# Weight maxima of two experts read from resident tiles, v's peeks two steps later, and a chunk's maximum set apart from its transposition

## The chip, the cores and the metric

One core of a Trainium2 chip runs one launch. The metric is device microseconds from the first to the last instruction of an execution, as the median of three runs. Five engines work side by side, each through its own queue and in the order of that queue: PE (TensorE, matrix products), DVE (VectorE), ACT (ScalarE), POOL (GpSimd) and SP, whose queue issues all transfers (DMAs) of this kernel. An instruction that has to wait holds back everything that stands behind it in its queue.

## What is computed

Causal attention with a decay per key for 4 batches of 8 heads (576 positions, 64 wide), and behind it a dense mixture of 4 experts over all 2304 tokens:

```python
scores = scale * np.matmul(q, k.transpose(0, 1, 3, 2))
scores = np.where(causal, -1000000000.0, scores + decay)
attn = softmax(scores)                      # over the keys
x = np.matmul(attn, v)                      # as 2304 tokens x 512
p = domain_probs / (domain_probs.sum(-1, keepdims=True) + 1e-09)
for e in range(4):
    h = np.maximum(x @ w1[e], 0.0)          # 512 -> 1024
    out += p[:, e:e + 1] * (h @ w2[e])      # 1024 -> 512
```

## The kernel before

**Chunks and steps.** The tokens are cut into 9 chunks of 256. Chunks 0 to 3 are the first 256 positions of a batch each, and chunks 4 to 8 share the other 320 positions of the four batches. The experts' work is a list of 80 steps. A step takes one chunk through two weight tiles (a tile is 128 hidden units of one expert, both matrices, 128x1024): `l1` (24 products, line 976) into PSUM, `gate` (ReLU into `gh` on ACT and the remainder `gl` on DVE, line 990), and one step later `l2` (12 products, line 1008); every second step DVE adds two PSUM tiles to `acc` (line 1031). Tile names carry the step as sweep, group, chunk and half: `l1_1_0_3_0` is the first half of group 0 of the second sweep for chunk 3. Steps 0 to 27 are the first sweep, with 32-bit tiles `wh` and `wl`, in which chunks 0, 1 and 2 go through the experts as they become ready. Steps 28 to 79 are the second sweep, in which chunks 1 to 4 go through with 16-bit halves; chunk 3 comes first in step 32 and chunk 4 in step 40. Chunks 5 to 8 follow in a last part (from about 650 us) with a scheme of their own, which the change does not touch.

**Attention beside the steps.** Attention for later chunks is a second list (`asteps`). Each entry has a cost, and `pace` hands entries out between the steps in proportion to these costs, so that a chunk is done three steps before its first use; `upto` hands out whatever is still missing when a step needs its chunk. For a head this is `s` (scores, line 608), a maximum on DVE (622), `p` (exponential on ACT, 637), for the second half of the positions `z` (16-bit halves, 702 and 703) and a transposing DMA from `z` to `pt` (708), and then `o` (attention times v, 783). When a chunk is complete, `turn(c)` finds its scale: `top` (a maximum over 128x1024 on DVE, line 257), `across` (a transposition on PE into `topx`, 196), `exponent` (DVE, and a second small product into `topx`, 217) and `finish` (DVE). `narrow` then makes the chunk's 16-bit halves `y` (ACT 471, DVE 472), which the second sweep's `l1` reads.

**Scales of weights and of v.** The second sweep also needs a power of two for each expert's two matrices and for v. Before, each expert gets 16 steps of `w_peek` (line 278): one DMA of 256 KB from HBM into `pk`, of which there is a single buffer, and one step later a maximum over it on DVE (281). `PEEK = (1, 15, 31, 45)` gives the first step for each expert. Then `w_scale` writes 128x2 maxima to HBM (`dw`) and reads them back to all partitions (`tops`, one buffer). For v there are ten `v_peek` steps (DMA of 512 KB into `vp`, maximum on ACT, 352) from step `V_PEEK = 1` on, and `v_scale` goes through HBM in the same way (`dv`, line 370, and `tops`, line 371).

```python
def w_peek(e, i):
    n, k = divmod(i, 2)
    t = pk_p.tile([128, 512], F32, tag="pk", name=f"pk{e}_{i}")
    nc.sync.dma_start(out=t, in_=w[8 * e + n, :, 512 * k : 512 * k + 512])
    at_step(step + 1, lambda: nc.vector.tensor_reduce(
        out=wmax[:, k, n, e : e + 1], in_=t, op=ALU.max, ...))
```

**What sets the order.** The program hands its instructions to a scheduler, which orders them for each engine before the launch (only the start-up part is ordered by hand). The order is then fixed. `w_split(n)` (line 897 issues the load of `wr`) turns a loaded tile into `wh` on ACT (line 916) and `wl` on DVE or POOL (920); in the first sweep tiles 16 to 23 are expert 2's (third) and 24 to 31 expert 3's (fourth), and all of them pass through SBUF there.

Of the kernel before, what the change touches and what calls it, by code (L numbers as in the profile page):

```python
# [8 lines left out]
F32 = mybir.dt.float32  # L9
# [4 lines left out]
ALU = mybir.AluOpType  # L14
AX = mybir.AxisListType
# [12 lines left out]
    ((1, 2, 3, 4), (1, 2, 3, 4), (2, 3, 4), (3, 4)),  # L28
)
WIDE = (0, 1, 2)  # L30
PEEK = (1, 15, 31, 45)
V_PEEK = 1
TURN = ((1, 14), (2, 18), (3, 24), (4, 28))
LEAD = 3
W_DVE = tuple(range(0, 16, 2))
# [41 lines left out]
def fused(ctx: ExitStack, tc: tile.TileContext, qk, v, f, probs, w, out):  # L77
    nc = tc.nc
# [35 lines left out]
    wmax = const.tile([128, 2, 8, E], F32, name="wmax")  # L114
# [72 lines left out]
    def at_step(n, f):  # L187
        later.setdefault(n, []).append(f)
# [54 lines left out]
    def x_scale(k, cols):  # L243

        def use(u, r):
            nc.vector.tensor_scalar(
                out=xsc[:, k : k + 1], in0=r, scalar1=2.0**2, scalar2=None, op0=ALU.mult
            )
            nc.vector.tensor_scalar(
                out=xun[:, k : k + 1], in0=u, scalar1=2.0**-2, scalar2=None, op0=ALU.mult  # L250
            )
            known.add(("x", k))

        def top():
            for i, c in enumerate(cols):
                x = xh[c].bitcast(F32) if c in WIDE else xf[c]
                nc.vector.tensor_reduce(
                    out=xmax[:, k + i : k + i + 1],
                    in_=x,
                    op=ALU.max,  # L260
                    axis=AX.XY,
                    apply_absolute_value=True,
                )
            n = len(cols)
            if n > 1:
                nc.vector.tensor_reduce(
                    out=xmax[:, k + n : k + n + 1], in_=xmax[:, k : k + n], op=ALU.max, axis=AX.X
                )

        n = k + len(cols) if len(cols) > 1 else k  # L270
        across, exponent, finish = power(1, xmax[:, n : n + 1], f"x{k}", use)
        return top, across, exponent, finish

    def w_peek(e, i):
# [8 lines left out]
            ),  # L283
        )

    def w_scale(e):

        def use(u, r):
            for k in range(2):
                nc.vector.tensor_scalar(  # L290
                    out=wsc[:, e, k : k + 1],
                    in0=r[:, k : k + 1],
                    scalar1=(2.0**2, 2.0**14)[k],
                    scalar2=None,
                    op0=ALU.mult,
                )
            nc.vector.scalar_tensor_tensor(
                out=wun[:, e : e + 1],
                in0=u[:, :1],
                scalar=2.0**-16,  # L300
                in1=u[:, 1:],
                op0=ALU.mult,
                op1=ALU.mult,
            )
            known.add(("w", e))

        m = st_p.tile([128, 2], F32, tag="wm", name=f"wm{e}", bufs=2)
        d = dr_p.tile([128, 2], F32, tag="dw", name=f"dw{e}", bufs=2)
        u = st_p.tile([128, 4], F32, tag="uw", name=f"uw{e}", bufs=2)

        def top():
            nc.vector.tensor_reduce(out=m, in_=wmax[:, :, :, e], op=ALU.max, axis=AX.X)
            nc.sync.dma_start(out=d, in_=m)
            nc.sync.dma_start(
                out=tops, in_=d.rearrange("q k -> (q k)").partition_broadcast(128)
            )

        def finish():
            nc.vector.tensor_reduce(
                out=u[:, :2],  # L320
                in_=tops.rearrange("p (q k) -> p k q", k=2),
                op=ALU.max,
                axis=AX.X,
            )
            nc.vector.tensor_scalar(
                out=u[:, :2], in0=u[:, :2], scalar1=TINY, scalar2=None, op0=ALU.max
            )
            nc.vector.tensor_scalar(
                out=u[:, :2].bitcast(I32),
                in0=u[:, :2].bitcast(I32),  # L330
                scalar1=EXPONENT,
                scalar2=None,
                op0=ALU.bitwise_and,
            )
            nc.vector.reciprocal(out=u[:, 2:], in_=u[:, :2])
            use(u[:, :2], u[:, 2:])

        return top, finish
# [141 lines left out]
    def turn(c):  # L480

        top, across, exponent, finish = x_scale(c, (c,))
        return [
            (50, lambda: (top(), across())),
            (50, exponent),
            (150, finish),
        ]

    class Job:
# [401 lines left out]
    wh, wl, wraw = {}, {}, {}  # L891
# [14 lines left out]
    def w_split(n):  # L906
        if n >= NS:
            if n % 2 == 0:
                big_split((n - NS) // 2)
            return  # L910
        w_load(n)
        r = wraw.pop(n)
        if n < 32:
            wh[n] = w_p.tile([128, 1024], F32R, tag="wh", name=f"wh{n}")
            wl[n] = w_p.tile([128, 1024], F32R, tag="wl", name=f"wl{n}")
            nc.scalar.activation(out=wh[n], in_=r, func=AF.Copy)  # L916
            eng = nc.vector if n in W_DVE else nc.gpsimd
            for a in (0, 512):
                z = a + 512
                eng.tensor_tensor(  # L920
                    out=wl[n][:, a:z],
                    in0=r[:, a:z],
                    in1=wh[n][:, a:z].bitcast(F32),
                    op=ALU.subtract,
                )
        else:
            e = n % 32 // 8
            assert ("w", e) in known
            t = w_pair(f"w{n}")
            wh[n], wl[n] = t[:, 0], t[:, 1]  # L930
            for k in range(2):
                c = slice(512 * k, 512 * k + 512)
                sc = wsc[:, e, k : k + 1]
                if k == 1:
                    nc.gpsimd.tensor_scalar(
                        out=r[:, c], in0=r[:, c], scalar1=sc, scalar2=None, op0=ALU.mult
                    )
                    nc.scalar.activation(out=wh[n][:, c], in_=r[:, c], func=AF.Copy)
                    nc.gpsimd.tensor_tensor(
                        out=wl[n][:, c], in0=r[:, c], in1=wh[n][:, c], op=ALU.subtract  # L940
                    )
                    continue
                nc.scalar.activation(out=wh[n][:, c], in_=r[:, c], func=AF.Copy, scale=sc)
                nc.vector.scalar_tensor_tensor(  # L944
                    out=wl[n][:, c],
                    in0=r[:, c],
                    scalar=sc,
                    in1=wh[n][:, c],
                    op0=ALU.mult,
                    op1=ALU.subtract,  # L950
                )
            at_step(step + 2, lambda: nc.sync.dma_start(out=wd[n - 32], in_=t))
        w_load(n + 1)
        w_load(n + 2)
        w_load(n + 3)
# [141 lines left out]
    def big_split(p):  # L1097
        if p >= 16:
            return
        r = wr_p.tile([128, 2, 512], F32, tag="wr", name=f"wr{NS + p}")  # L1100
        nc.sync.dma_start(
            out=r, in_=w[2 * p : 2 * p + 2, :, :512].rearrange("n p c -> p n c")
        )
        bw[p] = [w_pair(f"bw{p}_{k}") for k in range(3)]
        for k in range(2):
            nc.sync.dma_start(out=bw[p][k], in_=wd[2 * p + k])
        part = lambda b: r[:, b[0], 256 * b[1] : 256 * b[1] + 256]
        t = late.x.tile([128, 4, 256], F32, tag="wt", name=f"wt{p}", bufs=2)
        w_of = lambda b: part(b) if type(b) is tuple else t[:, b - 1, :]
        for k, a, z, op in SUMS:  # L1110
            nc.gpsimd.tensor_tensor(out=t[:, k - 1, :], in0=w_of(a), in1=w_of(z), op=op)
        f = t.rearrange("p k n -> p (k n)")
        hi, lo = bw[p][2][:, 0], bw[p][2][:, 1]
        nc.scalar.activation(out=f, in_=f, func=AF.Copy, scale=wsc[:, p // 4, 0:1])
        nc.scalar.activation(out=hi, in_=f, func=AF.Copy)  # L1115
        for a in (0, 512):
            z = a + 512
            nc.gpsimd.tensor_tensor(out=lo[:, a:z], in0=f[:, a:z], in1=hi[:, a:z], op=ALU.subtract)  # L1118
# [216 lines left out]
    prev, step = None, 0  # L1335
# [9 lines left out]
    for n in range(len(W_SLOT), 6):  # L1345
        w_split(n)

    used = set()
    for n in range(len(steps) + 1):
        step = n  # L1350
        cur = steps[n] if n < len(steps) else None
        for f_ in later.pop(n, ()):
            behind(f_)
        for e, first_ in enumerate(PEEK):
            if 0 <= n - first_ < 16:
                w_peek(e, n - first_)
            if n == first_ + 17:
                a_, b_ = w_scale(e)
                behind(a_)
                at_step(n + 3, b_)  # L1360
        if 0 <= n - V_PEEK < NV:
            v_peek(n - V_PEEK)
        if n == V_PEEK + NV + 1:
            a_, b_ = v_scale()
# [84 lines left out]
```

## Time and profile before

| | us |
|---|---|
| median of 3 runs | 965.07 |
| lowest and highest | 962.48 and 970.98 |
| the profiled execution | 969.94 |
| its span (first to last instruction) | 968.2 |
| mean granted TensorE clock in it | 0.981 of full speed |

The profile is that of one execution. Its time, 969.94 us, is 1.74 us more than its span, and 4.87 us above the median of the three runs. Times in the rows below count from the start of the span. Where a row says "A <- B", A's engine stood idle and B is what it waited for.

### The profile page before, as it was taken

What the parts mean: (1) busy time and instruction counts of PE and PEld (TensorE: products, weight loads), DVE (VectorE), ACT (ScalarE), POOL (GpSimd) and SP (SyncE); (2) the same over time, 40 slices, a digit from 0 to 9 for tenths busy, and PEclk for the clock granted to TensorE, in tenths of its full rate; (3) what the DMA queues carried; (4) which work ended last, traced back from release to release, by engine and by line L of the source; (5) the groups of instructions that cost most, each with busy time, mean ns of one, the idle gap of its engine ahead of it and who ended that gap; (6) DMA issues with size and microseconds to landing.
All of it is one profiled execution on the core that took longest, in us unless ns stands there. A gap on an engine that the chain in (4) does not pass through costs nothing.

```text
span 968.2 us, 15252 instructions
## 1 busy us (share of the span) xinstructions
PE 908.9 (94%) x5311; PEld 597.8 (62%) x5311; DVE 716.0 (74%) x1460; ACT 493.2 (51%) x983; POOL 441.6 (46%) x464
## 2 busy tenths in 40 slices
PE   4799998999989969899899989999999999999998
PEld 3699888999766647566566757654444444444443
DVE  5776775787978969789788878577666766676665
ACT  5777746466756748566666666454223222221110
POOL 4666955567624845425653564484233223320000
PEclk9999998999999969999999989999999999999999
DMA  7458753738987888975996599534122222121002
GB/s 245 141 200 288 263 125 132 207 109 288 256 194 180 228 191 209 275 156 141 278 345 141 111 257 292 121 120 151 65 87 75 100 66 81 50 66 44 1 1 88
DMA packets 130350, 154.13 MB, mean 159 GB/s; under 512 B 84868, under 2 KB 87616, under 8 KB 130272
## 3 DMA queue, kind: packets, MB, share of 16 engines
q1 hardware_dynamic: 130272, 153.14, 55.7%
q8 instruction: 42, 0.69, 0.3%
q14 instruction: 36, 0.29, 0.1%
HBM read 112.06 MB, written 21.65 MB: 138 GB/s over the span
## 4 chain that ended last, share of the span: by engine, by line
PE 58%; DMA 14%; DVE 12%; ACT 6%; POOL 5%; issue 4%; SPq 1%; ACTq 0%; DVEq 0%; POOLq 0%
PE y L1191 17%; PE m L1133 15%; PE l L1008 10%; PE l L976 9%; DMA pk<-in_w 4%; DMA raw<-in_qk 3%; DMA pt<-z 3%; PE s L608 3%; PE o L783 3%; DMA wr<-in_w 2%; DVE z L703 2%; DVE wmax L281 1%; DVE p L622 1%; DVE w L944 1%; ACT p L637 1%
## 5 line engine op out<-in xcount | busy, mean ns | idle before, releaser
L976 PE MATMUL l<-y,w 128*128 128x256 f16 x1248 | 157.2, 275 | 1.0 <-DVE y L472 1.0
L1191 PE MATMUL y<-bw,hh 128*128 128x512 f16 x512 | 152.3, 379 | 0.0
L637 ACT ACTIVATE p<-p,nm 128x576 f32<-128x576 f32 (+2 forms) x160 | 95.6, 598 | 93.3 <-DVE nm L622 93.0
L1133 PE MATMUL m<-rh,bw 128*128 128x512 f16 x448 | 139.3, 379 | 0.0
L976 PEld LDWEIGHTS <-w 128*128 128x128 f16 x1248 | 118.5, 99 | 33.4 <-issue 8.9
L1031 DVE SCALAR_TENSOR_TENSOR acc<-y,scg,acc 128x512 f32<-128x512 f32 x120 | 89.4, 749 | 59.7 <-PE y L1191 58.9
L1008 PE MATMUL l<-w,gh 128*128 128x512 f16 x416 | 127.3, 386 | 6.0 <-DVE acc L1031 6.0
L1118 POOL TENSOR_TENSOR bw<-wt,bw 128x512 f16<-128x512 f32 x32 | 36.7, 1171 | 176.4 <-ACT bw L1115 176.4
L1133 PEld LDWEIGHTS <-bw 128*128 128x128 f16 x672 | 65.7, 98 | 79.3
L1191 PE MATMUL y<-bw,hl 128*128 128x512 f16 x256 | 96.9, 379 | 0.0
L703 DVE SCALAR_TENSOR_TENSOR z<-p,z 128x384 f16<-128x384 f32 (+3 forms) x128 | 82.0, 661 | 17.9 <-ACT z L702 16.4
L608 PE MATMUL s<-hi 128*128 128x384 f32 (+1 forms) x192 | 77.5, 407 | 16.3 <-DVE hi L570 8.7
L1150 DVE TENSOR_TENSOR u<-m,u 128x512 f32<-128x512 f32 x96 | 65.7, 689 | 31.2 <-PE m L1133 29.3
L1191 PEld LDWEIGHTS <-hh 128*128 128x128 f16 x512 | 50.1, 98 | 60.4
L556 POOL CAST q<-raw 64x320 fp32r<-64x320 f32 (+1 forms) x56 | 26.4, 471 | 132.1 <-PE s L608 72.7
L1133 PE MATMUL m<-rl,bw 128*128 128x512 f16 x224 | 84.9, 379 | 0.0
L622 DVE CUSTOM_DVE_ANT_0 p<-s,mask 128x288 f32<-128x288 f32 (+2 forms) x160 | 74.5, 475 | 10.4 <-PE s L608 9.4
L1008 PE MATMUL l<-w,gl 128*128 128x512 f16 x208 | 79.5, 385 | 0.0
L1159 ACT ACTIVATE hh<-u 128x512 f16<-128x512 f32 x64 | 39.3, 626 | 78.5 <-DVE u L1150 78.5
L564 POOL TENSOR_TENSOR kl<-raw,hi 64x576 fp32r<-64x576 f32 (+1 forms) x56 | 66.9, 1195 | 25.6 <-ACT hi L555 25.5
L920 POOL TENSOR_TENSOR wl<-wr,wh 128x512 fp32r<-128x512 f32 x48 | 64.9, 1377 | 16.9 <-ACT wh L916 10.5
L990 DVE SCALAR_TENSOR_TENSOR gl<-l,gh 128x512 f16<-128x512 f32 (+1 forms) x80 | 54.7, 684 | 16.9 <-ACT gh L989 16.6
(154 smaller groups left out, 2031.3 us busy)
## 6 DMA issues: line engine op xcount, KB each, us to landing
wr<-in_w SPq DMA_DIRECT2D x80, 512.0 KB
pk<-in_w SPq DMA_DIRECT2D x64, 256.0 KB
wd<-w SPq DMA_DIRECT2D x32, 512.0 KB
bw<-wd SPq DMA_DIRECT2D x32, 512.0 KB
raw<-in_qk SPq DMA_DIRECT2D x16, 896.0 KB
raw<-in_qk SPq DMA_DIRECT2D x12, 512.0 KB
vp<-in_v SPq DMA_DIRECT2D x10, 512.0 KB
vr<-in_v SPq DMA_DIRECT2D x16, 320.0 KB
```

The source lines that it names most:

```text
L564: eng.tensor_tensor(out=kl[:64, :wk], in0=r[:64, ko : ko + wk], in1=hi[:64, ko : ko + wk].bitcast(F32), op=ALU.subtract,)
L608: nc.tensor.matmul(out=ps[:, at : at + z - a], lhsT=lhsT, rhs=rhs, start=(m == 0), stop=(m == 1),)
L622: nc.vector.tensor_tensor_reduce(out=pt[:, a:z], in0=ps, in1=mask[:, m0 + a : m0 + z], scale=-0.125, scalar=BIG if n == 0 else nm[:, col : ...
L637: nc.scalar.activation(out=pt[:, :w_], in_=pt[:, :w_], func=AF.Exp, scale=-1.0, bias=self.nmax[hh][:, c : c + 1], accum_out=self.ssum[:, h ...
L703: nc.vector.scalar_tensor_tensor(out=o[:, 1], in0=x, scalar=2.0**14, in1=o[:, 0], op0=ALU.mult, op1=ALU.subtract)
L920: eng.tensor_tensor(out=wl[n][:, a:z], in0=r[:, a:z], in1=wh[n][:, a:z].bitcast(F32), op=ALU.subtract,)
L976: nc.tensor.matmul(out=self.l1p[:, fi, :], lhsT=lhsT, rhs=rhs[:, k, :], start=(k == 0 and m == 0), stop=(k == 3 and m == 2),)
L1008: nc.tensor.matmul(out=l2[tt], lhsT=lhsT, rhs=rhs, start=(self.ps == 0 and fi == 0 and m == 0), stop=(self.ps == 1 and fi == 1 and m == 2),)
L1031: nc.vector.scalar_tensor_tensor(out=acc[c][:, tt, :], in0=ps, scalar=sc, in1=acc[c][:, tt, :], op0=ALU.mult, op1=ALU.add,)
L1133: nc.tensor.matmul(out=ps, lhsT=lhsT[:, o], rhs=rhs[:, k, :], start=(k == 0 and i == 0), stop=(k == 1 and i == 2),)
L1150: nc.vector.tensor_tensor(out=out, in0=a, in1=z, op=op)
L1191: nc.tensor.matmul(out=ps, lhsT=lhsT, rhs=rhs, start=(fi == 0 and m == 0), stop=(fi == 1 and m == 2),)
```

## The change

1. `PEEK` has only two entries, for experts 0 and 1. For experts 2 and 3 the 32 DMAs of 256 KB and their 32 maxima over 128x512 are gone. In their place `w_stat(n)` takes the maximum over the resident tile `wh[n]` (128x1024, two results) two steps after the tile is split, 16 times in all, and after the last tile of an expert `w_scale` follows.
2. `V_PEEK` goes from 1 to 3: v's peeks and its way through HBM come two steps later.
3. `turn` hands out `top` and `across` as two entries, and its four entries cost 450 together instead of 250.

```diff
-PEEK = (1, 15, 31, 45)
-V_PEEK = 1
+PEEK = (1, 15)
+V_PEEK = 3
@@
+    def w_stat(n):
+        nc.vector.tensor_reduce(
+            out=wmax[:, :, n % 8, n // 8],
+            in_=wh[n].bitcast(F32).rearrange("p (k f) -> p k f", k=2),
+            op=ALU.max, axis=AX.X, apply_absolute_value=True,
+        )
+        if n % 8 == 7:
+            top, finish = w_scale(n // 8)
+            at_step(step + 1, top)
+            at_step(step + 4, finish)
@@ def turn(c):
-            (50, lambda: (top(), across())),
-            (50, exponent),
-            (150, finish),
+            (100, top),
+            (150, across),
+            (100, exponent),
+            (100, finish),
@@ def w_split(n):
+            if n // 8 >= len(PEEK):
+                at_step(step + 2, lambda: w_stat(n))
```

The scheduler's order moves with it. Three places, each with the rows of one engine (line numbers of the changed kernel are up to 17 higher; numbers at the end of a name tell buffers apart).

DVE, where chunk 4's last attention head is added up (`xs`, `xf4`) and its maximum is taken; before:

```order
L990 SCALAR_TENSOR_TENSOR gl1_1_3_1_4603<-l1_1_1_3_1_4542,gh1_1_3_1_4602 128x512
L1031 SCALAR_TENSOR_TENSOR acc3_4168<-l2_1_1_3_0_0_4606,scg_130,acc3_4168 128x512
L281 TENSOR_REDUCE wmax_119<-pk2_8_4540 128x1
L1031 SCALAR_TENSOR_TENSOR acc3_4168<-l2_1_1_3_0_1_4613,scg_130,acc3_4168 128x512
L805 TENSOR_TENSOR xs0_3_1_4112<-o0_3_1_1_4251,tmp0_3_1_4111 64x320
L829 TENSOR_TENSOR xf4_3354<-xs0_3_1_4112,b0_3_1_4263 128x256
L829 TENSOR_TENSOR xf5_3356<-xs0_3_1_4112,b0_3_1_4263 128x64
L543 SCALAR_TENSOR_TENSOR v21_1_1_4430<-vr1_1_1_4133,vsc_123,v21_1_1_4430 128x10x64
L257 TENSOR_REDUCE xmax_125<-xf4_3354 128x1
```

and now:

```order
L820 TENSOR_TENSOR xs0_3_1_4149<-o0_3_1_1_4283,tmp0_3_1_4148 64x320
L1048 SCALAR_TENSOR_TENSOR acc3_4199<-l2_1_1_3_0_0_4617,scg_130,acc3_4199 128x512
L558 SCALAR_TENSOR_TENSOR v21_1_1_4463<-vr1_1_1_4170,vsc_123,v21_1_1_4463 128x10x64
L844 TENSOR_TENSOR xf4_3399<-xs0_3_1_4149,b0_3_1_4295 128x256
L844 TENSOR_TENSOR xf5_3401<-xs0_3_1_4149,b0_3_1_4295 128x64
L1048 SCALAR_TENSOR_TENSOR acc3_4199<-l2_1_1_3_0_1_4629,scg_130,acc3_4199 128x512
L257 TENSOR_REDUCE xmax_125<-xf4_3399 128x1
```

The maximum over the peeked tile `pk2_8` is gone from this place; the additions to `acc3` stand behind `xs` instead of ahead of it.

SP, where v's maxima go through HBM, with the loads of weight tiles 25 to 30 (`wr`); before:

```order
L278 DMA pk0_11_1947<-in_w 128x512
L370 DMA dv_1949<-vmax_122 128x1
L509 DMA vr2_3_0_1732<-in_v 128x256
L371 DMA tops_128<-dv_1949 128x128
L530 DMA kl2_3_0_0_1728<-ncd_131 2x256
L897 DMA wr25_1937<-in_w 128x1024
L897 DMA wr26_1944<-in_w 128x1024
```

and now, from the row behind `wr28`:

```order
L327 DMA dw2_2059<-wm2_2058 128x2
L278 DMA pk0_13_2166<-in_w 128x512
L384 DMA dv_2168<-vmax_122 128x1
L522 DMA raw2_3_0_1728<-in_qk 128x2x512
L328 DMA tops_128<-dw2_2059 128x256
L385 DMA tops_128<-dv_2168 128x128
L278 DMA pk0_14_2270<-in_w 128x512
L545 DMA kl2_3_0_1_1821<-ncd_131 2x256
L278 DMA pk1_0_2272<-in_w 128x512
L278 DMA pk0_15_2391<-in_w 128x512
L524 DMA vr3_0_0_1914<-in_v 128x256
L912 DMA wr29_2374<-in_w 128x1024
```

The loads of tiles 25 to 28 now stand ahead of both round trips, and 29 stands behind them. The two readings into `tops` follow each other; the second overwrites half of what the first brought for expert 2 before DVE reads it there, which changes that expert's power of two.

PE, from chunk 3's small products (`topx3`) to the first step with chunk 3; before (`...` leaves out 76 and 188 rows of steps 28 to 31):

```order
L196 MATMUL topx3_173<-ident_111,xmax_125 1x128
...
L217 MATMUL topx3_173<-ux3_174,ones_r_129 128x1
...
L1008 LDWEIGHTS gl1_0_2_0_3784
L1008 MATMUL l2_1_0_2_0_1_3888<-w33_3085,gl1_0_2_0_3784 128x512
L976 LDWEIGHTS w32_3077
L976 MATMUL l1_1_0_3_0_3905<-y3_3179,w32_3077 128x256
```

and now (`...` leaves out seven rows, three more products of `o` among them):

```order
L217 MATMUL topx3_173<-ux3_174,ones_r_129 128x1
...
L798 MATMUL o0_0_1_0_3242<-pt0_0_1_0_2989,v20_0_1_2900 128x64
L623 MATMUL s0_1_1_0_2_0_3291<-hi0_1_1_0_3093 128x384
L623 MATMUL s0_1_1_0_2_0_3291<-kl0_1_1_0_2908,q2_0_113 128x384
L623 MATMUL s0_1_1_0_3_0_3317<-hi0_1_1_0_3093 128x512
L623 MATMUL s0_1_1_0_3_0_3317<-kl0_1_1_0_2908,q2_0_113 128x512
L623 MATMUL s0_1_1_0_4_0_3349<-hi0_1_1_0_3093 128x288
L623 MATMUL s0_1_1_0_4_0_3349<-kl0_1_1_0_2908,q2_0_113 128x288
L623 MATMUL s0_1_1_0_4_1_3352<-hi0_1_1_0_3093 128x288
L623 MATMUL s0_1_1_0_4_1_3352<-kl0_1_1_0_2908,q2_0_113 128x288
L993 LDWEIGHTS w32_3104
L993 MATMUL l1_1_0_3_0_3942<-y3_3193,w32_3104 128x256
```

Between the second small product and the first product with chunk 3 there were about two and a half steps of work; now there are four products of `o` and eight of `s`.

## Rows read from the trace of the kernel before

**Rows 1.** Page, part 1: busy us, share of the span, instructions.

```profile
PE 908.9 (94%) x5311; PEld 597.8 (62%) x5311; DVE 716.0 (74%) x1460; ACT 493.2 (51%) x983; POOL 441.6 (46%) x464
```

**Rows 2.** Two stretches: length, busy us per engine, granted clock, DMA share, GB/s.

```profile
94.00:225.00 131.00, 125.61 (x838) 114.78 (x837) 92.38 (x229) 76.95 (x172) 83.97 (x94) 0.97 0.57 176
275.00:520.00 245.00, 221.47 (x1467) 151.85 (x1466) 203.08 (x467) 158.87 (x327) 121.56 (x115) 0.96 0.85 215
```

**Rows 3.** Who PE waited for, whole span: us in total, times, longest.

```profile
PE o L783 <- DMA pt<-z: 12.5, 7, 4.3
...
PE topx L196 <- DVE xmax L257: 7.2, 2, 6.9
...
PE o L783 <- ACT pth L737: 4.2, 1, 4.2
...
PE l L976 <- DVE y L472: 1.0, 1, 1.0
```

**Rows 4.** The same, from 270 to 300 us.

```profile
PE s L608 <- DVE xs L805: 1.6, 1, 1.6
PE o L783 <- DMA pt<-z: 1.3, 1, 1.3
PE s L608 <- DVE nm L622: 0.9, 2, 0.7
```

**Rows 5.** The same, from 455 to 500 us.

```profile
PE l L1008 <- DVE acc L1031: 3.4, 3, 1.8
```

**Rows 6.** Who DVE waited for, from 270 to 520 us.

```profile
DVE wmax L281 <- DMA pk<-in_w: 18.0, 10, 4.1
```

**Rows 7.** Chain of work, 120 to 175 us: start us, us, what.

```profile
129.99 7.54 DMA dv<-vmax
...
137.54 0.33 SPq L371
...
138.32 7.84 DMA wr<-in_w
...
148.27 0.58 PE o L783
```

**Rows 8.** Who ACT waited for, whole span.

```profile
ACT wh L916 <- DMA wr<-in_w: 9.5, 3, 8.5
```

**Rows 9.** Chain of work, 320 to 440 us.

```profile
343.42 4.06 DMA pk<-in_w
...
350.83 1.14 DVE xmax L257
352.01 0.39 PE topx L196
...
393.54 6.99 DMA pk<-in_w
400.56 0.69 DVE wmax L281
...
403.67 5.31 DMA pt<-z
...
409.12 2.13 PE o L783 x9
```

**Rows 10.** PE in three short stretches: length, PE busy us, granted clock, DMA share, GB/s.

```profile
148.00:154.00 6.00, 5.73 (x26) 0.58 0.37 125
352.00:366.00 14.00, 13.01 (x58) 0.55 0.58 142
408.00:414.00 6.00, 4.88 (x22) 0.72 0.79 194
```

**Rows 11.** DVE's maxima: line, count, ns min/median/max, first and last start us.

```profile
L281 DVE TENSOR_REDUCE wmax<-pk x64: 662/677/689, 58.8 to 519.8; 128x1 f32<-128x512 f32 x64
L257 DVE TENSOR_REDUCE xmax<-xf x6: 1209/1214/1215, 247.7 to 619.4; 128x1 f32<-128x1024 f32 x6
```

**Rows 12.** Who SP's queue waited for, whole span.

```profile
SPq L278 <- DVE wmax L281: 31.5, 25, 4.7
```

More of the change, by code (lines that the diff above doesn't have):

```diff
@@ L284, in w_peek @@
         )
+    def w_stat(n):
+        nc.vector.tensor_reduce(
+            out=wmax[:, :, n % 8, n // 8],
+            in_=wh[n].bitcast(F32).rearrange("p (k f) -> p k f", k=2),
+            op=ALU.max,
+            axis=AX.X,
+            apply_absolute_value=True,
+        )
[3 more added lines that the diff above has]
+            at_step(step + 4, finish)
     def w_scale(e):
```

## The prediction

> **What bounds the kernel now.** I began with the busy shares: PE works 94% of the span, DVE 74% [rows 1]. So most of the time can't move, and what a change can win or lose is where PE stands still, or runs at the lower of its two clock levels (1.2 instead of 2.4 GHz) after it stood still. Two stretches matter. From 94 to 225 us, in the first sweep, PE is busy 125.6 of 131 us and DVE 92.4. From 275 to 520 us PE is busy 221.5 of 245, so 23.5 us are idle, DVE 203.1, and the transfers are dense, 0.85 against 0.57 [rows 2]. Then I read who PE waits for [rows 3 to 5], followed the longest of these waits back through the chain [rows 7, 9], and read the clock behind them [rows 10]. Three stops stand out.
>
> - *At 148 us*, 4.2 us [rows 3]. The chain shows its origin on SP: v's maxima go to HBM in 7.54 us, SP waits for that before it may read them back, and the load of weight tile 25 stands behind it, issued at 138.32 and landing 7.84 us later [rows 7]. ACT waits 8.5 us for it [rows 8], and what PE needs stands behind that on ACT.
> - *At 352 us*, 6.9 us, before chunk 4's transposition, and 1.0 more before its first products [rows 3]. The chain is a peek of expert 2: its DMA starts at 343.42, DVE stands still until it lands, then takes `acc`, the last head's sums and chunk 4's maximum, and only then PE goes on [rows 9].
> - *At 409 us*, 4.3 us [rows 3]. Again a peek ahead of it: 6.99 us of DMA until DVE's maximum at 400.56, then `z`, then 5.31 us of transposing DMA [rows 9].
>
> In all, DVE waits 18.0 us for peeks between 270 and 520 us, in 10 waits [rows 6]. The single buffer works on SP too: 31.5 us of its queue's waits are a peek's DMA that waits for DVE to free the buffer [rows 12], and everything behind it, transposing DMAs included, waits along.
>
> Each stop costs clock as well. In 148 to 154 us the mean granted clock is 0.58, so 2 x 0.42 x 6 = 5.0 us ran at half speed; less 0.3 us idle, half of it is lost: 2.4 us. In the same way 352 to 366 us gives (2 x 0.45 x 14 - 1.0)/2 = 5.8, and 408 to 414 us (2 x 0.28 x 6)/2 = 1.7 at most, of which I take 1.4 since PE idles at its start [rows 10]. So the three stops are worth 6.6, 13.7 and 5.7 us.
>
> **The change part by part**, against the profiled execution's 969.94 us.
>
> *Peeks of experts 2 and 3 removed.* 32 maxima of 0.677 us leave DVE [rows 11], 21.7 us, nearly all after 275 us, and 32 DMAs of 256 KB, 8.4 MB, leave SP. DVE is not what PE waits for all the time, so I count waits, not work. (a) From 270 to 300 us the waits of PE add up to 1.6 + 1.3 + 0.9 = 3.8 us [rows 4], and DVE meets the first peeks of expert 2 there: -3.8, bounds 0 and -3.8. (b) Chunk 4: the DVE order shows the peek gone from between `gl` and the maximum. 4.06 us of the 6.9 us were its wait [rows 9]; 2.9 stay, since `acc` now stands among the sums and PE has a few products of `l2` to cover it. The 1.0 us before the first products stays. A stop of 2.9 + 1.0 = 3.9 us should cost clock like those of 4.2 and 4.3 us, 1.9 on average. 13.7 becomes 5.8: -7.9, bounds -4.1 (the wait alone) and -13.7. (c) At 409 us the peek's wait goes and the transposing DMA's own latency stays: I take 2.6 us of idle time and 1.0 of clock, -3.6, bounds 0 and -5.7. (d) From 455 to 500 us PE waits 3.4 us for `acc` [rows 5], with the eight last peeks in the queue: -1, bounds 0 and -3.4.
>
> *Maxima over resident tiles.* No row shows `w_stat`. The nearest is the chunk's maximum over as many elements, 1.21 us [rows 11]; two of the small maxima, 1.35 us, bound it from above. 16 x 1.21 = 19.4 us come onto DVE, nearly all between 94 and 225 us, where DVE goes from 92.4 to about 111 of 131 us [rows 2]. The order puts them right behind a `gl`, where the next `acc` still waits for PE; the work that hides them is PE's `l2` of the step before. They are not free: where they are late, `acc` is late, and then the next pair's `l2`, for want of PSUM. I take +2; bounds 0 and, if all of it landed on PE, +19.4.
>
> *v's way through HBM.* The SP order shows the loads of tiles 25 to 28 ahead of both round trips. So the stop at 148 us loses its cause: -6.6. Behind the round trips now stand the peeks 14, 0 and 15, and the load of tile 29. DVE must pass these peeks, ACT needs tile 29. I take +2, bounds 0 and +6.6, a stop like that at 148 us. The wait itself is known from one row, 7.54 us for a write of 0.5 KB [rows 7]. The Trainium skill ("DMA: Bandwidth & Descriptors", Anatomy of one DMA) puts a transfer's fixed cost, mostly the receipt of its write, at about 2.0 us, for the software queue. By that figure two round trips hold SP for some 4 us, tile 29 is in time, and this term would be 0; by the row it is not, and the sum goes by the row.
>
> *Order of attention.* With more on DVE in the first sweep, the scheduler lets attention for chunk 3 fall behind: in the new PE order 16 `s` products stand between steps 31 and 32, and chunk 3's second small product is four `o` and eight `s` ahead of its first use, where it was two and a half steps ahead. This is what chunk 4 already has, without a peek: its last wait was 1.0 us [rows 3], behind nine `o`. Five `o` fewer, at 2.13/9 = 0.24 us on the slow clock [rows 9], make 2.2 us; a transposing DMA behind it may add as much as one did at 297 us, 1.3 [rows 4]; clock some 1.5, since the stop is a little over half of those at 148 and 409 us. I take +5, bounds +1.0 and +13.7, chunk 4's whole stop.
>
> *Spacing of maximum and transposition.* For chunk 4 all entries are handed out together by `upto`, and the DVE order shows the maximum and what follows still back to back. Of the 7.2 us that PE waits for such maxima, 6.9 are chunk 4's [rows 3], so 0.3 is all there is to win elsewhere: 0. Its effect on pacing is in the term above.
>
> **Sum:** -3.8 - 7.9 - 3.6 - 1 + 2 - 6.6 + 2 + 5 = -13.9 us. Against the profiled execution that is 956.0, against the median, 4.87 us lower, 951.2. Whether the median's runs have all these stops at full length isn't known; I put the forecast between, at 953.
>
> **The rivals.** A measurement of this kernel can tell about 1% from no change, that is below 955.4 or above 974.7 us.
>
> *The stops are exchanged, not removed.* SP's two round trips hold tile 29 and the peeks as long as tile 25 was held (0 instead of -4.6), chunk 3 costs 2.2 + 1.3 + 2.4 + 2 = 7.9, chunk 4 loses just the wait (-4.1), 409 us just 2.6, (d) nothing, DVE costs +4 in the first sweep. With -3.8: 0 - 3.8 + 7.9 - 4.1 - 2.6 + 4 = +1.4, about 966 against the median. For it: in-order queues have handed such waits on before, as the chain at 148 us shows. Against it: DVE has 21.7 us less to do where most stops are.
>
> *PE runs through.* All named stops vanish: -6.6 - 3.8 - 13.7 - 5.7 - 3.4 and the lower bounds of the rest, +1: -32, about 933. Against it: the chain from a chunk's last head to its first products remains serial.
>
> *Slower: attention comes too late for both chunks.* PE's fixed order has chunk 3's and chunk 4's last heads closer to their use. If chunk 3 gets chunk 4's whole stop (+13.7), chunk 4's stays because its last `o` now waits for a transposing DMA of 5.3 us as at 403.67 [rows 9] (0 instead of -7.9), and six of the heads between wait 1.5 us each, like the 1.3 of [rows 4] and somewhat more (+9), then -3.8 - 2.6 + 2 - 6.6 + 2 + 13.7 + 9 = +13.7, about 979. It decides once chunk 3's stop is over 8 us and most heads wait. Against it: between steps 32 and 40 the number of `s` products is as before, 62.
>
> **Chances.** The forecast 0.50 (its own range 945 to 962), exchange 0.27, PE runs through 0.08, slower 0.15. Below 955.4 lie two thirds of the forecast's cases, the run-through and a few of the exchange: 0.45. Within 1%: 0.40. Slower: 0.15. For 8 in 10 the range reaches from 940, which leaves out most of the run-through, to 971, which leaves out most of the slower case.
>
> **What would show it.** Right: no idle time of DVE for `pk` after about 280 us; PE's wait before `topx` of chunk 4 near 3 us; no wait of ACT for a `wr` of tile 25 and no stop of PE near 148 us; 16 maxima of about 1.2 us before 250 us; a new wait of PE before chunk 3's first products, of 2 to 3 us. Wrong: a wait of ACT or DVE over 5 us behind `tops`; PE idle for more than 8 us in the first sweep; a stop of 5 us and more at chunk 3 with the clock at half; chunk 4's stop still at 6 us, now behind a `pt`.

## The result, and the profile after

The changed kernel is slower. Its median is 978.75 us over four runs (973.30 to 981.78) against 964.68 us of the kernel before; the ratio is 1.0115, with a 95% interval of 1.0076 to 1.0154. The forecast was 953 us, within 940 to 971. The profiled execution of the changed kernel took 981.78 us, 3.0 above its median.

The page's first part (busy us, share of the span, instructions) and then the two stretches of [rows 2], of the changed kernel:

```profile
PE 914.9 (93%) x5311; PEld 599.9 (61%) x5311; DVE 713.6 (73%) x1444; ACT 494.1 (50%) x983; POOL 436.3 (45%) x464
```

```profile
94.00:225.00 131.00, 122.17 (x780) 110.16 (x779) 99.04 (x218) 72.09 (x153) 76.76 (x86) 0.96 0.54 167
275.00:520.00 245.00, 222.64 (x1437) 150.53 (x1436) 192.11 (x450) 165.28 (x343) 129.59 (x125) 0.95 0.79 187
```

DVE does 11 us less between 275 and 520 us, half of the 21.7 us of maxima that left it there; other work has moved into the stretch. PE's idle time in it is 22.4 us (245 less 222.64), where it was 23.5. In the first sweep it grew from 5.4 to 8.8 us. DVE's busy time there rose by 6.7 us only, though sixteen new maxima of 1.21 us stand in it: 27 other instructions of DVE and 58 of PE fell out of the stretch and came later. Who PE waited for over the whole span, as in [rows 3] (lines are 14 to 17 higher than before):

```profile
PE l L1025 <- DVE acc L1048: 12.6, 8, 4.9
...
PE o L798 <- DMA pt<-z: 5.4, 6, 1.2
PE s L623 <- DVE nm L637: 4.7, 5, 2.9
PE l L993 <- ACT xh L850: 3.5, 2, 2.3
PE l L993 <- DVE y L486: 3.5, 2, 1.8
PE topx L196 <- DVE xmax L257: 3.4, 2, 2.8
PE o L798 <- ACT pth L752: 3.1, 1, 3.1
```

The two large waits of before, `pt` and `xmax`, have shrunk from 12.5 and 7.2 to 5.4 and 3.4 us; `acc`, `nm`, `xh` and `y` have grown. To compare stretches that hold the same work I cut both traces where `gl` of certain steps ends, and counted as loss PE's idle time plus what the lower clock level cost (busy time times one less the granted clock, in pieces of half a microsecond). The cut itself is good to some 2 us.

| loss in steps (us) | 0–11 | 11–21 | 21–27 | 27–36 | 36–41 | 41–50 | 50–62 | 62–79 | behind |
|---|---|---|---|---|---|---|---|---|---|
| before | 1.1 | 6.6 | 0.0 | 7.5 | 14.2 | 6.2 | 4.3 | 11.2 | 3.7 |
| after | 0.5 | 13.4 | 0.2 | 6.6 | 14.5 | 5.9 | 7.2 | 11.0 | 3.7 |

That is 54.9 against 63.1 us: 8.2 of the 11.8 us between the two spans (the start-up, which the change does not touch, is 1.6 us longer in this execution). Of the 8.2 us, 6.4 came in the first sweep (to step 27), and in the second, where the gain was forecast, there is none. In the first sweep the stop at 148 us is gone, and three others stand behind its place; with their clock they cost 4.8, 4.5 and 3.7 us. Who PE waited for from 126 to 215 us, and the windows (length, PE busy, PEld, DVE, ACT, POOL, granted clock, DMA share, GB/s) behind the three:

```profile
PE o L798 <- ACT pth L752: 3.1, 1, 3.1
PE s L623 <- DVE nm L637: 2.9, 1, 2.9
PE l L993 <- ACT xh L850: 2.3, 1, 2.3
```

```profile
158.00:164.00 6.00, 5.28 (x27) 4.84 (x28) 2.91 (x9) 4.86 (x10) 5.07 (x7) 0.72 0.26 82
188.00:194.00 6.00, 5.19 (x22) 4.48 (x23) 4.70 (x13) 2.68 (x8) 2.00 (x3) 0.72 0.24 73
202.00:208.00 6.00, 5.96 (x36) 5.71 (x37) 3.74 (x9) 0.93 (x2) 0.00 (x0) 0.72 0.08 22
```

Each of them is followed by some microseconds at the lower clock level, as after the stops of before [rows 10]. The chain of work (start us, us, what) leads from the first of them to the round trips:

```profile
146.91 0.38 SPq L384
147.38 10.17 DMA raw<-in_qk
...
158.20 0.48 ACT pth L752
158.72 0.38 PE o L798
```

Right behind v's write (L384) SP issued the next head's `raw`, and that took 10.17 us; ACT stood 8.2 us for it. Before, it was weight tile 25 with 7.84 us [rows 7]. The second stop, at 188 us, has a peek behind it, and expert 0's round trip ahead of that: SP wrote its maxima at 180.42 us and went on

```profile
183.18 0.33 SPq L328 DMA_DIRECT2D tops<-dw  x1
183.63 5.27 SPq L278 DMA_DIRECT2D pk<-in_w  x2
```

DVE stood 4.0 us for the first of these peeks, and the maximum `nm` that PE needed stood behind it. In the kernel before, a weight tile followed this read-back, not a peek. The third stop, `xh` at 202 us, is chunk 2's last head, which comes late.

### The profile page after: what moved, and what is told of

Same layout as the page of the kernel before. It is cut to its first block, busy times and chain, and to the rows that moved or that the text cites. A ratio compares the mean times of both kernels' runs of the same rounds, so it can differ in the third digit from the quotient of the medians.

```text
span 980.0 us, 15237 instructions
## 1 busy us (share of the span) xinstructions
PE 914.9 (93%) x5311; PEld 599.9 (61%) x5311; DVE 713.6 (73%) x1444; ACT 494.1 (50%) x983; POOL 436.3 (45%) x464
## 4 chain that ended last, share of the span: by engine, by line
PE 50%; DVE 18%; DMA 13%; ACT 7%; issue 5%; POOL 5%; SPq 0%; ACTq 0%; DVEq 0%; POOLq 0%
PE y L1208 17%; PE m L1150 15%; PE l L1025 7%; PE l L993 7%; DMA raw<-in_qk 6%; DMA pk<-in_w 4%; DVE z L718 3%; DVE p L637 2%; DVE acc L1048 2%; PE s L623 2%; ACT p L652 2%; PE o L798 2%; DVE gl L1007 1%; DMA pt<-z 1%; ACT z L717 1%
## 5 line engine op out<-in xcount | busy, mean ns | idle before, releaser
L579 POOL TENSOR_TENSOR kl<-raw,hi 64x576 fp32r<-64x576 f32 (+1 forms) x56 | 64.9, 1159 | 23.5 <-ACT hi L570 23.5
```

Of the source, the lines that this page charges most:

```text
L579: eng.tensor_tensor(out=kl[:64, :wk], in0=r[:64, ko : ko + wk], in1=hi[:64, ko : ko + wk].bitcast(F32), op=ALU.subtract,)
```

## The experiments

Times are medians; the ratio is to the kernel before on the same chip, whose medians were 965.5 to 966.9 us. "Constant" means that the maxima of experts 2 and 3 are left out of the computation and a constant stands for them.

| kernel | us | ratio (95%) |
|---|---|---|
| e1: maxima from tiles alone | 978.4 | 1.0117 (1.0078–1.0157) |
| e2: v and turn alone | 977.1 | 1.0113 (1.0086–1.0141) |
| e16: v alone | 969.3 | 1.0036 (1.0010–1.0062) |
| e8: turn alone | 973.1 | 1.0071 (1.0043–1.0100) |
| e5: before without peeks 2 and 3, constant | 967.4 | 1.0013 (0.9994–1.0031) |
| e3: after, round trips in steps 48, 62 | 968.7 | 1.0015 (0.9984–1.0046) |
| e14: after, round trips in steps 44, 58 | 966.6 | 1.0006 (0.9983–1.0029) |
| e13: after, round trips in steps 34, 46 | 973.7 | 1.0080 (1.0055–1.0105) |
| e15: after, round trips in steps 22, 28 | 983.3 | 1.0185 (1.0150–1.0220) |
| e4: after without maxima, constant | 973.9 | 1.0075 (1.0047–1.0103) |
| e6: e4 with trips in 48, 62 | 967.0 | 1.0018 (0.9991–1.0044) |
| e7: e1 with trips in 48, 62 | 976.8 | 1.0128 (1.0083–1.0173) |
| e9: after, read-backs apart | 976.6 | 1.0109 (1.0081–1.0137) |
| e10: before, read-backs apart | 961.5 | 0.9961 (0.9940–0.9983) |
| e17: e10 without peeks 2 and 3, constant | 961.3 | 0.9944 (0.9925–0.9963) |
| e18: e3 with read-backs apart | 966.1 | 0.9996 (0.9970–1.0022) |
| e11: e8, small product held early | 969.4 | 1.0037 (1.0016–1.0058) |
| e12: e1, small product held early | 981.9 | 1.0149 (1.0101–1.0198) |

**The parts apart.** Each is the kernel before with some hunks of the change's diff: e1 those of `PEEK`, `w_stat` and `w_split`; e8 that of `turn`; e16 (below) that of `V_PEEK`; e2 the last two.

> Part 1 of the change alone: maxima of experts 2 and 3 from the resident tiles, v's peeks and turn as before. Theory A (the 16 maxima on DVE hold attention back in the first sweep, so that it comes late for chunks 1, 2 and 3): nearly the whole loss is here, 974 to 980 us, and DVE or ACT waits at the first use of chunk 2 stay. Theory B (v's round trip has moved next to expert 2's, and the two together hold SP): here v's trip is where it was, so under 970 us, but with a stop near 148 us as before. Theory C (the loss comes from turn's new costs): as the kernel before or better, 955 to 965.

> Parts 2 and 3 alone: v's peeks two steps later and turn's new entries and costs, with the peeks of experts 2 and 3 as before. Theory A: within 1% of the kernel before, 960 to 970 us. Theory B: also within 1%, since expert 2's round trip is not next to v's here. Theory C: 974 us and more.

> Part 3 alone: turn's four entries and costs, everything else as before. The order of PE hardly differs from before in the first sweep; attention is about 4 products later between steps 35 and 38. If the loss of 10.6 us of parts 2 and 3 together is turn's: 974 to 978. If it is v's: 963 to 968.

e8, at 973.1 us, lies just under its first expectation. The losses don't add up: 11.9 us for the maxima, 10.6 for v and turn (3.2 and 6.2 alone), and 14.1 for all three together. None of the theories A to C was right alone: A is right on e1 and wrong on e2, C the other way round, and B is wrong on both, though right on e3 and e4 below.

**What the peeks are worth.** This is the gain on which the forecast rested.

```diff
-            if 0 <= n - first_ < 16:
+            if e < 2 and 0 <= n - first_ < 16:
```

> The kernel before without the peeks of experts 2 and 3 (32 DMAs of 256 KB and 32 maxima): this part of the computation is left out, and a constant stands for their maxima; nothing is put in its place, round trips, turn and v as before. It prices the gain on which the prediction rested. The prediction's terms (3.8 + 7.9 + 3.6 + 1 = 16.3 us): about 950 us. Theory D (the chains from one attention head to the next run through ACT and the transposing DMAs as well, so that DVE's time in them is not what ends them; the stops stay with another last link): 961 to 967 us.

It is nothing that can be measured: 967.4 us against 966.8, with an interval that leaves room for 1 us of gain at most. Who DVE waited for from 270 to 520 us, the rows beside [rows 6], of the kernel before, and then of the one without peeks:

```profile
DVE wmax L281 <- DMA pk<-in_w: 18.0, 10, 4.1
DVE z L703 <- ACT z L702: 6.8, 6, 2.2
DVE gl L990 <- ACT gh L989: 3.5, 4, 2.2
DVE xs L805 <- ACT tmp L797: 3.0, 4, 1.0
```

```profile
DVE z L704 <- ACT z L703: 21.5, 22, 4.1
DVE gl L991 <- ACT gh L990: 11.7, 5, 4.2
DVE xs L806 <- ACT tmp L798: 8.4, 3, 4.5
```

The 18.0 us for `pk` are gone, and the waits for ACT (`z`, `gh`, `tmp`) rise from 13.3 to 41.6 us. Much of the time in which DVE had stood at the peek it now stands for ACT. For PE it is similar; who it waited for around chunk 4 (steps 36 to 41), before and without peeks:

```profile
PE topx L196 <- DVE xmax L257: 6.9, 1, 6.9
PE l L976 <- DVE y L472: 1.0, 1, 1.0
PE l L1008 <- DVE acc L1031: 0.4, 1, 0.4
```

```profile
PE l L977 <- ACT y L472: 4.0, 1, 4.0
PE s L609 <- DVE xf L830: 1.7, 1, 1.7
PE l L1009 <- ACT gh L990: 1.5, 1, 1.5
PE topx L197 <- DVE xmax L258: 1.4, 1, 1.4
PE o L784 <- DMA pt<-z: 1.2, 1, 1.2
PE l L977 <- DVE y L473: 1.0, 1, 1.0
```

One stop of 6.9 us became six of 1.0 to 4.0. They cost less clock: the loss in steps 36 to 50 fell from 20.4 to 14.1 us. But in steps 50 to 62 it rose from 4.3 to 9.3, so that what was won at chunk 4 was for the most part lost behind it. In that run the order had also put chunk 4's second small product behind nine products of attention and v. So e17 holds that product early and starts from the quieter first sweep of e10:

> The kernel before with read-backs apart (961.5 us) and without the peeks of experts 2 and 3 (left out, a constant stands for their maxima), chunk 4's second small product held ahead of the nine products of attention and v. In the run without peeks that product had slipped behind them, so that a gain of the peeks could have been hidden. If it was hidden there: 952 to 957 us. If the stops at chunk 4 and behind are not DVE's, with or without peeks: 959 to 964.

961.3 us, with peeks 961.5 (e10, on another chip): again nothing clear of the error (0.2 us by the medians, 1.6 by the ratios), now with 8.4 MB and 32 maxima less. The loss shows the same exchange: against e10, steps 36 to 50 lose 14.1 us instead of 23.5, and steps 50 to 62 lose 12.5 instead of 5.4 (a hint only, since e10's profiled execution, 966.4 us, is 4.9 above its median and e17's is 1.0 below).

**v's way, and what stands behind a small write.**

> Part 2 alone, v's peeks and trip two steps later. The prediction's reading: tiles 25 to 28 are loaded ahead of the trip, the stop at 148 us goes and the time falls by up to 6.6, to 959 to 963 us. The other reading: another load stands behind the trip instead, and a stop of 4 to 5 us comes near 157 us, as in all runs with v two steps later so far: 966 to 971 us.

The stop moves from 148 to 157 us and stays 3.9 us long. SP's queue in e16 (start us, us, what), then DVE's longest wait, then transfers in pieces of 3 us (the last three numbers are granted clock, DMA share, GB/s):

```profile
145.26 0.38 SPq L370 DMA_DIRECT2D dv<-vmax  x1
147.72 0.33 SPq L278 DMA_DIRECT2D pk<-in_w  x1
148.15 0.37 SPq L897 DMA_DIRECT2D wr<-in_w  x1
154.30 0.33 SPq L371 DMA_DIRECT2D tops<-dv  x1
```

```profile
DVE wmax L281 <- DMA pk<-in_w: 7.3, 2, 5.5
```

```profile
145.00:148.00 3.00, 3.00 (x24) 2.87 (x23) 1.19 (x4) 1.54 (x4) 3.00 (x5) 1.00 0.97 325
148.00:151.00 3.00, 3.00 (x20) 2.57 (x19) 1.63 (x3) 1.41 (x3) 1.99 (x4) 1.00 1.24 85
151.00:154.00 3.00, 2.15 (x18) 1.95 (x16) 0.00 (x0) 0.00 (x0) 1.36 (x2) 1.00 0.38 26
```

Here SP does not wait: a peek and a weight tile are in the queue 3 us behind v's write, 768 KB together, and yet 26 GB/s move from 151 to 154 us, and DVE stands 5.5 us for the peek. So not only what SP withholds is late, but also what it has issued. (The DMA share counts a transfer's whole length where it starts, so it can pass 1.) In e10 and e9 the read-back is queued some loads later, behind a peek's DMA:

```diff
             nc.sync.dma_start(out=d, in_=m)
-            nc.sync.dma_start(out=tops[:, :128], in_=...)
+        def back():
+            with tc.issue_after(peeked[-1].ins):
+                nc.sync.dma_start(out=tops[:, :128], in_=...)
@@
             behind(a_)
-            at_step(n + 2, b_)
+            at_step(n + 2, r_)
+            at_step(n + 4, b_)
```

> The kernel before with the same separation of write and read-back, v's above all; the other engines' order is the same as before. The stop at 148 us is 4.2 us and 2.4 us of clock. If it is removed, 966.8 - 6.6 = 960 us. If stops are only exchanged (the next in-order wait shows up a few steps later): 964 to 968.

> The changed kernel with each trip through HBM in two parts: the write, and the read-back two or three steps later, queued behind the last peek's DMA, so that SP doesn't stand still between them (chunk 4's second small product keeps its place behind eight score products). If the loss in steps 14 to 21 is SP standing still for two trips in a row: the stops near 158 and 188 us shrink (loss in steps 11 to 21 from 13.4 to about 7) and the time falls to 968 to 972 us, as with the late trips (968.7). If it is not the wait on SP but the lag of attention: 976 to 980.

e10, together with e17, which contains it, is the one clean gain: 961.5 us, faster than both kernels, 4.0 of the 6.6 us expected. The loss in steps 11 to 21 falls from 6.6 to 0.0; who PE waited for from 94 to 225 us:

```profile
PE l L984 <- ACT xh L843: 0.6, 1, 0.6
PE s L616 <- DVE nm L630: 0.6, 1, 0.6
PE topx L196 <- DVE xmax L257: 0.3, 1, 0.3
```

The transfers stay slow behind v's write there too:

```profile
133.50:136.50 3.00, 3.00 (x21) 2.75 (x20) 2.52 (x5) 3.00 (x8) 3.00 (x3) 1.00 0.91 31
136.50:139.50 3.00, 3.00 (x22) 2.77 (x22) 3.00 (x4) 1.19 (x2) 2.96 (x3) 1.00 0.22 31
```

but tile 25 is now issued at 134.98 us instead of 138.32, and PE has work until it is there. In the changed kernel the same edit gives nothing clear of the error (e9, 976.6): its loss in steps 11 to 21 falls from 13.4 to 9.4, and steps 27 to 36 take it back (6.6 to 10.9).

**When the round trips come.** In e3 and e13 to e15 the maxima stay where the change puts them; only the steps of the trips of experts 2 and 3 move.

```diff
-            at_step(step + 1, top)
-            at_step(step + 4, finish)
+            late = (48, 62)[n // 8 - 2]
+            at_step(late, top)
+            at_step(late + 3, finish)
```

> The changed kernel, but experts 2 and 3 go through HBM in steps 48 and 62 as before the change; the maxima stay in the first sweep. Theory A: still 973 to 979 us, since the maxima are what holds attention back. Theory B: the stop near 158 us is gone (6 us with its clock), and that near 188 us may go too: 964 to 970 us. Theory C: as the changed kernel, 978.

> The same with steps 44 and 58. Early round trips as the cause: 966 to 971 us. A fortunate order as the cause: scatter, 966 to 979, and the runs at 34, 44 and 48 differ among each other by more than 5 us.

> The changed kernel with the round trips of experts 2 and 3 in steps 34 and 46, so after v's trip and after the first sweep, but not where the kernel before has them. If early round trips are what costs 10 us: 966 to 971 us, as with steps 48 and 62 (968.7). If the run with steps 48 and 62 was only a fortunate order: anywhere from 966 to 979.

> The same with steps 22 and 28: still in or at the end of the first sweep, but well behind v's trip. If it is the two trips next to each other on SP: 967 to 971 us, with a loss of 7 to 9 us in steps 11 to 21. If any trip in the first sweep costs: 974 to 979.

With trips in the second sweep: 966.6, 968.7 and 973.7 us; with early ones 978.8 and 983.3. So in the changed kernel early trips cost about 5 to 17 us, and it isn't that they stand next to v's (e15 stands apart and is the slowest; its loss is in steps 27 to 36, 19.4 us against 6.6). e13 lies outside its first expectation and e15 outside both. With v and turn as before, the same move gives hardly anything: 978.4 against 976.8 us (e1 and e7). So this price is not one of the trips alone. The scatter among the three late ones, 7 us for the same work, is the measure of what a mere reordering does here. Why early trips cost so much is not settled: SP standing still between write and read-back is no clear part of it (e9), and slow transfers behind each trip are a candidate that no run isolates.

**What the maxima cost.** e4 takes them out of the changed kernel; e6 is e4 with e3's edit, e7 is e1 with e3's edit, and e18 is e3 with the read-backs apart and chunk 4's small product held early (below).

```diff
     def w_stat(n):
-        nc.vector.tensor_reduce(out=wmax[:, :, n % 8, n // 8], in_=wh[n]..., op=ALU.max, ...)
         if n % 8 == 7:
```

> The changed kernel without the 16 maxima over the resident tiles: this part of the computation is left out, and a constant stands for the maxima of experts 2 and 3. The round trips through HBM stay where the change put them. Theory A: the first sweep loses its lag, and the gain of the missing peeks is seen: 955 to 965 us. Theory B: the stops near 158 and 188 us stay: 968 to 976 us. Theory C: 974 us and more.

> The changed kernel without the 16 maxima (left out, a constant stands for them) and with the round trips of experts 2 and 3 in steps 48 and 62. If maxima and round trips are the two prices of the change and add up (4.8 and 10.0 us by the medians of the two runs that lack one of them): 978.8 - 14.8 = 964 us. If v's later way and turn's costs are a price of their own, as the run of these two alone says (977.1, 10.6 over before): 970 us and more. By the prediction's gain of 16.3: 950.

> The maxima from the resident tiles with the round trips in steps 48 and 62, v and turn as before. If the loss of 10.6 us by v and turn alone holds here too: 968.7 - 10.6 = 958 us, better than both kernels. If v and turn lose only beside the peeks of experts 2 and 3: 966 to 972.

> The changed kernel with round trips of experts 2 and 3 in steps 48 and 62, all read-backs apart and chunk 4's second small product held early: the best form of the change that the runs point to. If v's trip is the only loss of the run with late trips that can be removed (5 of its 7.3 us in steps 11 to 21): 963 to 966 us. If the maxima's lag decides (chunk 2's first product waits 3.2 us): 966 to 971. Better than the kernel before with read-backs apart (961.5) by neither.

Without the maxima the changed kernel is 4.8 us faster (e4), which is hardly clear of the error, and with late trips 1.8 (e6 against e3), which is not. The place is visible: the wait for `xh` at chunk 2's first product in step 20, 2.3 us in the changed kernel, is 2.3 to 3.3 in every run with both the maxima and v two steps later, and absent without the maxima (e4, e6) and with v as before (e1, e7). e6 came between its expectations. e7 was missed by both: 976.8 us, with a loss of 21.2 us in steps 36 to 41, where chunk 4's small product stands behind nine products of attention and v. e18 lies between its two expectations, at 966.1 us; its loss in steps 11 to 21 is still 7.3, with 3.0 us of waiting near 156 us and 2.5 for `xh`. That is the kernel before again, not better.

**Where chunk 4's second small product stands.** In e1, e2, e7 and e8 the order moved it behind nine `o` (in e5 and e6 as well); in the kernels before and after it is ahead of them. So nothing of what this place costs is in the changed kernel's own 14.1 us.

```diff
         def av(self, hh):
-            self.av_pe(hh)
+            if (self.nm, hh) == ("1_0_1", 0):
+                with tc.issue_after(small["x4"].ins):
+                    self.av_pe(hh)
+            else:
+                self.av_pe(hh)
```

> Part 3 alone, as in the run of turn alone (973.1 us), but PE's order at chunk 4 is held as in the kernel before: the second small product of its scale stands behind eight score products, ahead of nine products of attention and v (o), not behind them. If this place is what turn costs: 966 to 969 us, and the loss in steps 36 to 41 falls from 20.0 to about 14. If turn's cost lies elsewhere: 972 to 974.

> Part 1 alone, as in its run (978.4 us), with chunk 4's second small product held ahead of the nine products in the same way. If the place is worth what the profile shows (a loss of 21.3 us in steps 36 to 41 against 14.2): 971 to 973 us. If maxima and round trips carry the whole loss: 977 to 980.

Who PE waited for around chunk 4, turn alone (336 to 374 us), then with the product held early (336 to 376):

```profile
PE topx L196 <- DVE xmax L257: 5.0, 1, 5.0
PE l L977 <- ACT y L471: 4.5, 1, 4.5
PE o L784 <- DMA pt<-z: 3.3, 1, 3.3
```

```profile
PE topx L198 <- DVE xmax L259: 4.9, 1, 4.9
PE l L983 <- DVE y L474: 2.6, 1, 2.6
PE l L1015 <- DVE acc L1038: 1.3, 1, 1.3
PE topx L219 <- DVE ux L212: 1.2, 1, 1.2
```

That gives 2 to 4 of turn's 6.2 us (2.3 by the differences on each chip, 3.7 by the medians), at the edge of the error. For e12 it gave nothing: 981.9 against 978.4; the loss at chunk 4 fell from 21.3 to 17.7, and 50 to 79 rose from 8.6 to 15.1. Both expectations, 971 to 973 and 977 to 980, were wrong. So a loss that one place shows is again not what its removal gives back.

## Why the prediction was wrong

*Most of the signs it named came, and the sum was wrong.* DVE waits for no peek after 280 us. PE's wait ahead of `topx` for chunk 4 is 2.8 us (3 forecast). ACT waits 1.8 us for tile 25, where it waited 8.5, and no stop stands at 148 us. The sixteen maxima take 1.21 us each:

```profile
L288 DVE TENSOR_REDUCE wmax<-wh x16: 1200/1211/1216, 106.1 to 219.9; 128x2 f32<-128x1024 f32 x16
```

Chunk 3 stops for 0.4 + 0.5 + 0.9 + 1.8 us and loses 2.9 to the clock, 6.6 in all (5 forecast). But a sign that one stop is gone says nothing of the next. Two of the four signs of being wrong came too: PE idles 8.8 us in the first sweep (8 named), and ACT stands 8.2 us for a load between the writes and the read-backs (over 5 behind `tops` was named). The forecast's terms beside the loss that changed, by stretch:

| steps | terms of the sum (us) | forecast | loss after less before |
|---|---|---|---|
| 0–27 | v's way -6.6 + 2, maxima +2 | -2.6 | +6.4 |
| 27–36 | (a) -3.8, attention +5 | +1.2 | -0.9 |
| 36–41 | (b) | -7.9 | +0.3 |
| 41–50 | (c) | -3.6 | -0.3 |
| 50–62 | (d) | -1.0 | +2.9 |
| 62 on | none | 0 | -0.2 |
| sum | | -13.9 | +8.2 |

Only the term for chunk 3 and (a) came out. Two steps failed: the gain of the peeks in (b) to (d), and the price of the first sweep.

*Peeks removed (-16.3).* This is the larger of the two steps that failed. It took a wait of DVE that the chain named, and gave PE its whole length back. e5 and e17 measure nothing clear of the error. Term (b) made 13.7 us into 5.8 at chunk 4; the loss in steps 36 to 41 went from 14.2 to 14.5, in more and shorter stops (the waits for `acc`, `pt` and `y` stand where the peek stood). Term (c): the stop of 4.3 us at 409 us is one of 1.1 at 416 us now, but stops of 1.6 and 1.9 us came up at 426 and 450 us, and 0.3 us were gained, not 3.6. Term (d): the wait for `acc` at 474 us grew to 3.0 us with 2.8 of clock. The chain shows what ended last, not what would have ended next: in e5 six stops of 1.0 to 4.0 us took the place of one.

*v's way (-6.6 + 2).* The reading of the order was right, tile 25 is ahead. But the cause was read only in part. It is not only that SP waits: the transfers behind the round trip are slow as well, so whoever stands there is late. It was tile 25, then `raw` (10.17 us), in e16 a peek. The +2 for this was mis-sized: the two stops at 158 and 188 us cost 9.3 us with their clock, over the upper bound of 6.6. The price of 2.0 us that the Trainium skill ("DMA: Bandwidth & Descriptors", Anatomy of one DMA) gives as fixed cost was rightly not used: the rows have 7.54 us before, and in the changed kernel SP stood 6.7 us ahead of the second read-back.

*Maxima (+2).* The duration was right to 0.01 us. They did not make PE wait where the prediction looked, at the next `acc`; attention fell behind in the first sweep, chunk 2's last head included (the prediction looked at chunks 3 and 4). Taking them out gives 1.8 us with late trips and 4.8 with early ones, so +2 is not refuted. The round trips of experts 2 and 3, which moved with the maxima into the first sweep, have no term beyond the +2 of v's way: with these trips put later the changed kernel is 5 to 12 us faster (e13, e3, e14).

*Turn (0).* Alone it costs 6.2 us. The costs move entries against each other, and with them the place of a product of 0.2 us for which chunk 4's halves `y` wait. In the changed kernel that product keeps its place, and what turn costs there no run shows.

*The rivals.* The slower one had nearly the right time, 979, for the wrong reason: chunk 3 did not take chunk 4's stop. What it did have was chunk 4's stop staying. The exchange had the right mechanism, but counted in it only stops that the profile of before showed; its 966 is near what e3, e14 and e18 reach (966 to 969), where the early trips are taken out. That the measured time lies at the slower rival's 979 is luck.

## What to carry to other kernels

Where the path alternates between engines, the wait that a chain names can be the last of several, and the next ones take its place. Before a removed wait is booked as a gain, read what the same engine waits for one instruction later, and test the gain with the cheapest kernel that has nothing in its place, as e5. And where a scheduler makes the order, a reordering alone is worth some 7 us here, as much as the effects that are sought; several variants of one idea tell more than one.

A small result that goes through HBM and back should be written early, and read back some loads later, so that nothing urgent stands behind the write; that alone was worth 0.4% in the kernel before; in the changed kernel it gave nothing clear.

## What was not expected of the hardware

Around a round trip of 0.5 KB (128 rows of 4 bytes) transfers are slow, also loads that are already issued: 26 GB/s in e16 from 151 to 154 us and 31 GB/s in e10 from 133.5 to 139.5, both behind the write, where 325 GB/s had moved in e16 from 145 to 148 us. The transfer engines' share is 1.24 in e16 from 148 to 151 us at 85 GB/s, so they are occupied and move little. The Trainium skill ("DMA: Bandwidth & Descriptors", Specifications) says that transfers below 512 bytes are done by reading and writing back; the rows agree that tiny rows are slow, but that large loads behind them are slow too is only in these traces. No run here changes the size of the rows, and not every small write shows such a stretch: behind expert 2's at 422.7 us in the kernel before, 282, 185 and 149 GB/s move in the next three pieces of 3 us. Nor is it the write alone. In the kernel before SP had already waited for it when the read-back and tile 25 were issued (from 137.5 us), and from 139 to 142 us only 31 GB/s moved at a share of 0.86, before 354 GB/s moved from 142 to 145. What makes it stays open.
